# Linear attention, routed experts and a gated layer in one kernel: compact attention state, keys transposed after scaling, fewer spare zones zeroed, w_out's first words loaded into the slot's row tile

## The chip, the cores and the metric

The kernel runs on one core of a Trainium2 chip. The metric is device time of one execution in microseconds (us). TensorE is called PE, VectorE DVE, ScalarE ACT, GpSimd POOL, and SyncE SP; SP issues nearly all DMAs of this kernel, POOL the indirect ones.

## The reference

Three layers follow one another on 3072 tokens (4 batches of 768), with 384 features each:

```python
# 1: attention with a decaying state, 8 heads of 48
for t in range(S):
    cur = einsum('bhd,bhe->bhde', u * k[t], v[t])
    y[t] = einsum('bhd,bhde->bhe', r[t], state + cur)
    state = w[:, :, None] * state + einsum('bhd,bhe->bhde', k[t], v[t])
# 2: one of 8 experts for each token
e_idx = argmax(x @ w_gate + modality_bias[modality_id], axis=1)
out[mask] = gate_w[mask] * (relu(x[mask] @ w1[e]) @ w2[e])
# 3: gated layer with RMS norm
xn = x / sqrt(mean(x * x) + 1e-6) * rms_g
out = (silu(xn @ w_gate) * (xn @ w_val)) @ w_out
```

The weights of layer 3 are 64-bit floats; the kernel reads their two 32-bit words and makes a high and a low part of 32 bits from them.

## The kernel before

**Attention** works on 24 tiles of 128 tokens (i = 0 to 23; batch i % 4, chunk i // 4). The step loop at L833 is a software pipeline written out by hand: step s_ takes the state of tile s_-2 (`a_state`), transposes r and k of tile s_+1 (`a_T`, PE) and scales them with powers of w (`a_scale`, DVE), loads tile s_+4, multiplies keys with rows for tile s_ (`a_A`, PE), masks them (`a_mask`, DVE), forms y of tile s_-1 and the state's increment (`a_Y`, PE, copy on ACT), prepares the diagonal of tile s_+2 (`a_diag`, DVE, then eight ACT instructions), products with k for tile s_+3 (`a_rk`, `a_kp`, POOL), and turns y of tile s_-2 into token rows with gate logits (`a_X`). The order on PE, DVE, ACT, POOL and SP within the loop is that of the code. `soft()` puts the next small DVE instruction of routing behind an attention instruction; `hard()` drains what is left of it and issues the rank matmuls.

State `St[b]` is 128 partitions by 8 heads by 64, with each second head's half of the partitions zero, so that `pair(St[b], q)` is a full 128 by 128 matrix (L755). It is updated in two halves of 64 partitions: two DVE adds (L782) and two POOL products (L784). Keys are transposed unscaled from the padded load buffer (L718) and scaled by DVE out of PSUM (L726). `kpad` holds the keys times `Qt`, which POOL makes at L696 for the state's increment. Heads are padded from 48 to 64, and the pad columns are cleared by POOL.

**Hand-over to the experts.** `a_X` writes a token's row into one of six tiles `x` (L659). Routing finds, three tiles at a time, each token's place in the table `xs` in HBM, and POOL scatters one tile a step (`send_one`, L242). `xs` has for each expert 800 spare rows (`ZONE`) ahead of its tokens, which must read as zero when an expert's last slot reaches into them. SP writes zeros there during the step loop: the dummy zone in step 3, and one expert's zone in every second step from 5 to 19 (`zero_rows`, L257), 9 in all.

**Experts** work on slots of 792 tokens: two early slots, whose expert is known after 15 tiles, two more that are always computed, and a loop for any further ones. SP reads a slot's rows into `xslot` (L552), ACT scales them by the gate (L560), PE transposes them, and w1 and w2 come in chunks of 256 through three buffers each (L541, L543). A list of PE steps sets the order (one up and one down matmul group for a block of 128 hidden units and half a slot); from step 13 on pieces of layer 3's weights are decoded beside it (`decode`, L269). y goes to `ys` in HBM.

**Layer 3** (`glu`, L1095) takes blocks of 512 tokens: `gather` reads them from `ys` into `z`, `norm` scales them, `gv` makes the gated product for 128 hidden units, `o_mm` multiplies with w_out. In the first block, w_out's chunk f-1 is decoded in turn f; its words are loaded two turns ahead into a two-buffer staging tile, from the entry of `glu` on (L1148). z has one buffer; the next block's norm is spread over turns 1 to 10, its first ACT squares standing behind turn 1.

Of the kernel before, what the change touches and what calls it, by code (L numbers as in the profile page):

```python
# [24 lines left out]
E = 8  # L25
# [15 lines left out]
G = 3  # L41
EARLY_T = 15
# [14 lines left out]
def moe_chain_kernel(ctx: ExitStack, tc: tile.TileContext, r, k, v, w, u, mod, wgate, mbias,  # L57
# [34 lines left out]
    def pad_tile(nm, n, pool):  # L92
# [5 lines left out]
        P.memset(t[:, :, D:64], 0.0)  # L98
# [148 lines left out]
    def body(fast):  # L247
        with ExitStack() as st:
            moe = ExitStack()
            mp = moe.enter_context(tc.tile_pool(name="mp", bufs=2))  # L250
            zrow = {}

            def zero_rows(e):
                if not zrow:
                    zrow[0] = tabs[0:ZONE // 10, KD * HALF:KD * HALF + XW]
                    P.memset(zrow[0], 0.0)
                d = SP.dma_start(out=xs[e * STRIDE:e * STRIDE + ZONE, :].rearrange("(p t) d -> p t d", t=10),  # L257
                                 in_=zrow[0].rearrange("p (t d) -> p t d", t=1).to_broadcast([ZONE // 10, 10, XW]))
                if e < E:
                    tc.declare_no_dep(d.ins, group="xs", reason="rows that no token has")  # L260
                    tc.add_to_no_dep_group("xs", d.ins)
# [50 lines left out]
            def route(g, ls, xt):  # L312
# [40 lines left out]
                bk = bank(7, "rank")  # L353
                rk = bk[:, 0:G * E]
                T.matmul(rk, tri16, M.rearrange("p g e -> p (g e)"), start=True, stop=False)
                T.matmul(rk, ones16, C[:, 0:G, :].rearrange("p g e -> p (g e)"), start=False, stop=True)
                if (g + 1) * G in (EARLY_T, NT):
                    T.matmul(bk[0:1, 128:128 + E], ones16[:, 0:1], C[:, G, :], start=True, stop=True)
# [12 lines left out]
                if (g + 1) * G in (EARLY_T, NT):  # L371
                    cnt = p.tile([1, E], F32, name="cntf")
                    V.tensor_copy(cnt, bk[0:1, 128:128 + E])
# [133 lines left out]
            def slot_memory():  # L507
# [4 lines left out]
                return r1, r2, mp.tile([SUB, NSUB, XW], F32, name="xslot", bufs=1)  # L512

            raws1, raws2, xrows = slot_memory()
# [135 lines left out]

            def a_X(i):
# [6 lines left out]
                if fast:  # L658
                    x = xt[i] = ap.tile([128, XW], F32, name="x", bufs=6)  # L659
# [627 lines left out]
```

## Time and profile before

| what | us |
|---|---|
| median of 3 runs (lowest, highest) | 906.7 (905.68, 914.93) |
| the profiled execution | 903.63 |
| its span, first to last instruction | 901.8 |
| PE busy | 828.4 (92%) |
| DVE, ACT, POOL busy | 478.5, 332.8, 267.5 |
| mean granted PE clock | 0.968 |

The profile is of one execution. A line of the trace gives the start in us from the span's start, the duration, the engine, the line of the kernel, the operation and its output and inputs; in brackets stand the engine's idle time ahead of it and what ended it. PE's matmuls overlap, so the distance between starts says more than a duration. The granted clock is 1.00 at 2.4 GHz, and 0.50 at 1.2 GHz. The DMA share is the mean busy share of the 16 DMA engines.

### The profile page before, as it was taken

The numbers are of one execution on the slowest core, as the hardware profiler recorded it, in microseconds if no ns is written. First come the engines' busy times: TensorE is split into PE (matmuls) and PEld (weight loads), VectorE is DVE, ScalarE is ACT, GpSimd is POOL, SyncE is SP. The second block draws the span as 40 slices with busy tenths as digits, with TensorE's granted clock in tenths as the row PEclk, the third lists the DMA queues.
The fourth block names the chain that finished last, engine by engine and source line by source line (L and its number), as shares of the span: only waits on it lengthen the run. The fifth ranks groups of instructions, "written<-read, shape, count | busy, mean of one in ns | idle before, by whom it ended". The sixth has DMA issues, their size and how long they took to land.

```text
span 901.8 us, 13427 instructions
## 1 busy us (share of the span) xinstructions
PE 828.4 (92%) x5097; PEld 751.5 (83%) x5097; DVE 478.5 (53%) x969; ACT 332.8 (37%) x731; POOL 267.5 (30%) x314
## 2 busy tenths in 40 slices
PE   6996686988999999999699999999999999999995
PEld 5885576878989899999587888888888888888885
DVE  8985667848565787654178635324423423532121
ACT  3563244554655546543333331231222223122111
POOL 6453445634334234322154430120111013011001
PEclk9998798989999999999899999999999999999998
DMA  9999685275574364560711200110100010000001
GB/s 133 186 210 215 144 207 145 90 193 148 175 243 134 121 203 119 115 113 30 117 54 55 86 36 1 36 36 1 34 28 9 1 36 36 1 1 35 1 1 39
DMA packets 120831, 80.40 MB, mean 89 GB/s; under 512 B 85142, under 2 KB 111534, under 8 KB 120750
## 3 DMA queue, kind: packets, MB, share of 16 engines
q1 hardware_dynamic: 117470, 69.91, 32.6%
q0 software_dynamic: 3072, 9.46, 2.9%
q8 instruction: 43, 0.70, 0.4%
q14 instruction: 38, 0.31, 0.2%
q10 hardware_dynamic: 208, 0.00, 0.0%
HBM read 53.91 MB, written 25.46 MB: 88 GB/s over the span
## 4 chain that ended last, share of the span: by engine, by line
PE 53%; DMA 13%; issue 13%; DVE 10%; ACT 5%; POOL 4%; SPq 0%; POOLq 0%; ACTq 0%; DVEq 0%
PE vb L1116 11%; PE gb L1116 11%; PE hp L611 8%; DMA xs<-x,pos_all 7%; PE ob L1131 4%; PE ob L1132 4%; PE ob L1130 4%; PE y L630 2%; PE y L631 2%; PE y L629 2%; DMA kpad<-k 1%; DMA raw<-moe_w_gate 1%; DVE w1l L53 1%; DVE Am L743 1%; PE xb L656 1%
## 5 line engine op out<-in xcount | busy, mean ns | idle before, releaser
L1120 DVE TENSOR_TENSOR sg<-sg,vb 128x512 f32<-128x512 f32 x72 | 49.5, 687 | 216.8 <-PE vb L1116 211.7
L1130 PE MATMUL ob<-woh,acth 128*128 128x384 f32 x288 | 97.7, 339 | 6.5 <-ACT woh L285 6.5
L1131 PE MATMUL ob<-wol,acth 128*128 128x384 f32 x288 | 98.2, 341 | 2.6 <-POOL wol L53 2.5
L1122 ACT ACTIVATE acth<-sg 128x512 fp32r<-128x512 f32 x72 | 45.5, 632 | 148.6 <-DVE sg L1120 148.6
L1132 PE MATMUL ob<-woh,actl 128*128 128x384 f32 x288 | 97.7, 339 | 0.0
L1119 ACT ACTIVATE sg<-gb 128x512 f32<-128x512 f32 x72 | 42.8, 595 | 132.3 <-PE gb L1116 132.3
L711 ACT ACTIVATE Am<-ident,cd 128x128 f32<-128x128 f32 x184 | 56.4, 389 | 53.4 <-DVE cd L704 53.4
L611 PE MATMUL hp<-xh,w1h 128*128 128x396 f32 x192 | 68.5, 357 | 3.8 <-DVE hl L616 2.2
L242 POOL DMA_INDIRECT out<-room,toks x24 | 23.2, 966 | 155.1 <-ACT room L1141 84.3
L611 PE MATMUL hp<-xh,w1l 128*128 128x396 f32 x192 | 66.5, 346 | 2.4 <-DVE w1l L53 2.4
L611 PE MATMUL hp<-xl,w1h 128*128 128x396 f32 x192 | 66.2, 345 | 0.2 <-DVE xl L584 0.2
L630 PE MATMUL y<-hl,w2h 128*128 128x396 f32 x192 | 65.6, 342 | 0.8 <-DVE hl L616 0.8
L629 PE MATMUL y<-hh,w2h 128*128 128x396 f32 x192 | 65.6, 341 | 0.3 <-ACT hh L614 0.3
L631 PE MATMUL y<-hh,w2l 128*128 128x396 f32 x192 | 65.7, 342 | 0.0
L53 DVE TENSOR_TENSOR actl<-sg,acth 128x512 fp32r<-128x512 f32 x60 | 41.5, 692 | 41.9 <-ACT acth L1122 41.9
L1130 PEld LDWEIGHTS ob<-woh,acth 128*128 128x128 f32 x288 | 54.6, 190 | 10.0 <-ACT woh L285 7.1
L1131 PEld LDWEIGHTS ob<-wol,acth 128*128 128x128 f32 x288 | 54.4, 189 | 7.7 <-POOL wol L53 5.3
L616 DVE SCALAR_TENSOR_TENSOR hl<-hp,hh 128x396 fp32r<-128x396 f32 x64 | 36.2, 566 | 40.5 <-ACT hh L614 40.5
L1132 PEld LDWEIGHTS ob<-woh,actl 128*128 128x128 f32 x288 | 54.5, 189 | 0.1
L614 ACT ACTIVATE hh<-hp 128x396 fp32r<-128x396 f32 x64 | 32.0, 499 | 44.8 <-PE hp L611 44.5
L656 PEld LDWEIGHTS xb<-tabs,yT 128*128 128x128 f32 x192 | 27.2, 217 | 24.1 <-DVE ls L668 12.8
L1116 PE MATMUL gb<-xh,wgh 128*128 128x512 f32 x108 | 42.5, 394 | 1.9 <-issue 1.9
(258 smaller groups left out, 2114.7 us busy)
## 6 DMA issues: line engine op xcount, KB each, us to landing
xs<-tabs SPq DMA_DIRECT2D x9, 1206.2 KB
room<-moe_w SPq DMA_DIRECT2D x26, 384.0 KB
raw<-moe_w SPq DMA_DIRECT2D x14, 384.0 KB
xslot<-xs SPq DMA_DIRECT2D x8, 597.1 KB
raw<-moe_w_gate SPq DMA_DIRECT2D x12, 384.0 KB
raw<-moe_w_val SPq DMA_DIRECT2D x12, 384.0 KB
z<-ys SPq DMA_DIRECT2D x6, 768.0 KB
raw<-moe_w_out SPq DMA_DIRECT2D x12, 384.0 KB
```

What stands on the lines that cost most here:

```text
L53: eng.tensor_tensor(out, a, h.bitcast(F32), op=ALU.subtract)
L611: T.matmul(hp[:, 0:HALF], l[:, kk, :], m[:, kk], start=(n == 0), stop=(n == 8))
L629: T.matmul(y, bh[:, sl], hh, start=(f == 0), stop=False)
L630: T.matmul(y, bh[:, sl], hl, start=False, stop=False)
L631: T.matmul(y, bl[:, sl], hh, start=False, stop=(f == NFE - 1))
L711: A.activation(am[i][:, h % 2, h // 2, :], ident, AF.Copy, scale=c_[:, h:h + 1])
L1116: T.matmul(dst, l, m[:, kk], start=(n == 0), stop=(n == 8))
L1120: V.tensor_tensor(sg, sg, vb, op=ALU.mult)
L1122: A.activation(ah, sg, AF.Copy)
L1130: T.matmul(ob[o][:, 0:DM], ah[:, sl], wo_h[f], start=(f == 0), stop=False)
L1131: T.matmul(ob[o][:, 0:DM], ah[:, sl], wo_l[f], start=False, stop=False)
L1132: T.matmul(ob[o][:, 0:DM], al[:, sl], wo_h[f], start=False, stop=(f == NF2 - 1))
```

## The change

St becomes 128 partitions by 4 head pairs by 64; it is updated on all partitions by one DVE and one POOL instruction, and y takes from it two 64 by 64 products a pair in place of one of 128 by 128. From tile 2 on PE transposes `kpad` (keys already scaled), and ACT copies the result out of PSUM. Loaded keys then need no cleared pad beyond the first two buffers. y alternates between two PSUM banks; the increment s and the rank matmuls share bank 5. The ring of x rows has 10 tiles. Only the dummy zone is zeroed in the step loop; the zones of the two later slots' experts are zeroed when these slots are known. The words of w_out go into the memory of `xslot`, four chunks deep, and the first four are asked for during the last expert unit; the table for Silu is asked for at the entry of `glu`.

```diff
+XB = 10
...
-        P.memset(t[:, :, D:64], 0.0)
+        if nm != "k" or n < 2:
+            P.memset(t[:, :, D:64], 0.0)
...
+            xrow_t = xrp.tile([128, NSUB, XW], F32, name="xslot")
+            raw_o = xrow_t.rearrange("p t d -> p (t d)")[:, 0:8 * DM].bitcast(I32)
...
+            def zero_zone(sl):
+                SP.dma_start(out=xs[0:E * STRIDE, :].rearrange("(e n) d -> e n d", e=E)[bass.ds(sl.e, 1), 0:ZONE, :]
+                             .rearrange("o (p t) d -> p (o t) d", t=10), in_=zsrc)
...
+            def wo_load(f):
+                SP.dma_start(out=raw_o[:, f % 4], in_=o2w[f * 128:(f + 1) * 128, :].rearrange("p (n two) -> p n two", two=2))
...
-                bk = bank(7, "rank")
-                rk = bk[:, 0:G * E]
+                rk = aux[:, A_RK:A_RK + G * E]
...
-                    x = xt[i] = ap.tile([128, XW], F32, name="x", bufs=6)
+                    x = xt[i] = ap.tile([128, XW], F32, name="x", bufs=XB)
...
-                St = [ac.tile([128, H, 64], F32, name=f"St{b}") for b in range(B)]
+                St = [ac.tile([128, NP, 64], F32, name=f"St{b}") for b in range(B)]
...
+                        src = padded(nm, i) if nm == "r" or i < 2 else kpad[i % 5]
                         for q in range(NP):
-                            T.transpose(tb[:, q * 128:(q + 1) * 128], pair(padded(nm, i), q), ident)
+                            T.transpose(tb[:, q * 128:(q + 1) * 128], pair(src, q), ident)
...
-                        V.tensor_tensor(t, tb.rearrange("p (q n) -> p q n", q=NP), tab, op=ALU.mult)
                         tr[i].append(t)
-                        soft()
+                        if nm == "kT" and i >= 2:
+                            A.activation(t.rearrange("p q n -> p (q n)"), tb, AF.Copy)
+                        else:
+                            V.tensor_tensor(t, tb.rearrange("p (q n) -> p q n", q=NP), tab, op=ALU.mult)
+                            soft()
...
-                    y = bank(4, "y")
+                    y = bank(7 if i % 2 else 4, "y")
                     if c:
                         for q in range(NP):
-                            T.matmul(y[:, q * 128:(q + 1) * 128], pair(St[b], q), rT[:, q, :],
-                                     start=(q == 0), stop=False, skip_group_check=True)
+                            for hf in range(2):
+                                sl = slice(64 * hf, 64 * hf + 64)
+                                T.matmul(y[sl, q * 128:(q + 1) * 128], St[b][sl, q, :], rT[sl, q, :],
+                                         start=(q == 0), stop=False, skip_group_check=True)
...
-                        for n in range(2):
-                            rows = slice(64 * n, 64 * n + 64)
...
+                            tmp = ap.tile([128, NP, D], F32, name="stmp")
+                            V.tensor_tensor(tmp, sp, sf, op=ALU.add)
+                            soft()
+                            P.tensor_tensor(sf, tmp, decay, op=ALU.mult)
...
                     if s_ == 3:
-                        zero_rows(E)
-                    if 5 <= s_ < 5 + 2 * E and s_ % 2:
-                        zero_rows((s_ - 5) // 2)
+                        zero_row()
+                        zero_dummy()
...
                         slots.append(slot_new(rt["tabR"], j))
+                        zero_zone(slots[-1])
...
+                if n == len(units) - 1 and q == 6:
+                    for i in range(4):
+                        wo_load(i)
...
+                    A.activation(warm, ones[0:1, 0:1], AF.Silu)
...
-                    wo_load(0)
-                    wo_load(1)
                     gather(1)
...
-                        for _ in decode(raws.pop(f), wo_h[f], wo_l[f], DM):
+                        for _ in decode(raw_o[:, f % 4], wo_h[f], wo_l[f], DM):
                             pass
-                        if f + 2 < NF2:
-                            wo_load(f + 2)
+                        if f + 4 < NF2:
+                            wo_load(f + 4)
```

SP's queue in the step loop, around steps 3 to 5, before (L104 loads r, k and v of a tile, `room` and the names with `pad` are their buffers; L257 writes zeros to a zone of `xs`):

```order
L257 DMA xs<-tabs 800x1x386
L104 DMA rpad_203<-r 128x8x48
L104 DMA kpad_205<-k 128x8x48
L104 DMA room<-v 128x8x48
L104 DMA room<-r 128x8x48
L104 DMA room<-k 128x8x48
L104 DMA vpad_201<-v 128x8x48
L257 DMA xs<-tabs 800x1x386
L104 DMA room<-r 128x8x48
```

and with the change, the same place of SP's queue:

```order
L265 DMA xs<-tabs 800x1x386
L106 DMA rpad_206<-r 128x8x48
L106 DMA kpad_208<-k 128x8x48
L106 DMA room<-v 128x8x48
L106 DMA room<-r 128x8x48
L106 DMA room<-k 128x8x48
L106 DMA vpad_204<-v 128x8x48
L106 DMA room<-r 128x8x48
L106 DMA room<-k 128x8x48
```

The dummy zone stays, and the zone after six more loads is gone; so it is seven more times in the loop.

SP's queue in the second expert unit, before (`tabfb` is the table of the later slots, L541 and L543 load chunks of w1 and w2, L643 writes y of half a slot):

```order
L541 DMA raw_0_177<-moe_w 128x3x256
L543 ISA
L543 DMA raw_0_178<-moe_w 128x2x384
L526 TENSOR_LOAD tabfb
L526 ISA x2
L526 TENSOR_LOAD tabfb
L526 ISA x2
L541 ISA
L541 DMA room<-moe_w 128x3x256
L643 DMA ys<-tabs 128x3x396
L543 ISA
L543 DMA room<-moe_w 128x2x384
```

and with the change, the same place:

```order
L557 DMA raw_0_182<-moe_w 128x2x384
L540 TENSOR_LOAD tabfb
L540 ISA x2
L269 ISA
L269 DMA xs<-tabs 800x1x386
L657 DMA ys<-tabs 128x3x396
L540 TENSOR_LOAD tabfb
L540 ISA x2
L269 ISA
L269 DMA xs<-tabs 800x1x386
L555 ISA
L555 DMA room<-moe_w 128x3x256
```

Two zones of zeros now stand ahead of the next chunk of w1 (`room`), and so does the write of `ys`, which followed that chunk before.

ACT at the end of the step loop, before (`Am` is the diagonal, x a row tile, yT the copy of y, and the `xslot` rows scale the first slot's rows by the gate):

```order
L711 ACTIVATE Am<-ident,cd 128x128 x8
L660 ACTIVATE x<-xb 128x384
L591 ACTIVATE w1h<-raw_0_177 128x384
L762 ACTIVATE yT<-y 128x512
L600 ACTIVATE w2h<-raw_0_178 128x384
L660 ACTIVATE x<-xb 128x384
L591 ACTIVATE w1h<-raw_0_177 128x384
L762 ACTIVATE yT<-y 128x512
L560 ACTIVATE xslot<-xslot 99x384 x4
L660 ACTIVATE x<-xb 128x384
```

and with the change:

```order
L748 ACTIVATE kT<-kTp 128x512
L605 ACTIVATE w1h<-raw_0_181 128x384
L614 ACTIVATE w2h<-raw_0_182 128x384
L605 ACTIVATE w1h<-raw_0_181 128x384
L787 ACTIVATE yT<-y 128x512
L729 ACTIVATE Am<-ident,cd 128x128 x8
L678 ACTIVATE x<-xb 128x384
L748 ACTIVATE kT<-kTp 128x512
L574 ACTIVATE xslot<-xslot 99x384 x4
L787 ACTIVATE yT<-y 128x512
L678 ACTIVATE x<-xb 128x384
L787 ACTIVATE yT<-y 128x512
```

kT stands ahead of each yT. Four of the slot's eight scalings, which stood behind the last yT before, have moved up ahead of the yT of tile 21.

## Rows read from the trace of the kernel before

**Rows 1.** Busy time by window: engines, granted clock, DMA share and GB/s
```profile
core 0: us, PE busy (x) PEld busy (x) DVE busy (x) ACT busy (x) POOL busy (x), PEclk, DMA share, GB/s
0.00:24.40 24.40, 16.17 (x138) 13.69 (x138) 21.47 (x51) 8.66 (x25) 13.78 (x40) 0.94 0.95 135
24.40:60.00 35.60, 33.03 (x436) 30.13 (x437) 32.51 (x88) 21.71 (x66) 18.83 (x28) 1.00 1.03 199
60.00:101.50 41.50, 27.10 (x312) 24.67 (x309) 21.44 (x58) 13.58 (x41) 13.42 (x20) 0.86 0.98 208
...
161.00:174.00 13.00, 13.00 (x166) 11.78 (x164) 12.33 (x38) 6.81 (x21) 9.18 (x13) 0.99 0.41 136
...
220.00:236.00 16.00, 14.86 (x82) 14.86 (x83) 11.50 (x30) 8.74 (x19) 4.57 (x5) 1.00 0.92 275
```

**Rows 2.** DMA issues by line: engine, operation, count, size of one
```profile
xs<-tabs SPq DMA_DIRECT2D x9, 1206.2 KB
```

**Rows 3.** Who waited for whom, 24 to 188 us: total, times, longest
```profile
POOL St L784 <- DMA xs<-x,pos_all: 42.8, 9, 9.1
...
ACT x L660 <- DMA xs<-x,pos_all: 28.6, 8, 7.5
...
PE xb L656 <- DVE ls L668: 12.0, 6, 5.9
PE rank L356 <- DVE C L342: 11.3, 6, 2.3
```

**Rows 4.** The tile x, 24 to 188 us: its scatters from issue to landing
```profile
DMA to landing us min/median/max: 2.7/5.9/10.8
```

**Rows 5.** Timeline of PE, one step of attention without waits
```profile
163.76 1.14 PE L656 MATMUL xb<-tabs,yT 128*128 128x104 f32 x8
...
165.71 0.37 PE L736 MATMUL Aa<-rT,kT 64*128 64x128 f32 x1
...
166.59 0.27 PE L736 MATMUL Ab<-rT,kT 64*128 64x128 f32 x1
166.80 1.16 PE L755 MATMUL y<-rT,St 128*128 128x128 f32 x8
167.88 1.09 PE L759 MATMUL y<-Am,room 128*64 128x128 f32 x16
...
169.36 0.36 PE L656 MATMUL xb<-tabs,yT 128*128 128x104 f32 x1
```

**Rows 6.** The chain that ended last, one round through DVE and ACT
```profile
41.87 0.60 DVE kT L726
...
42.56 1.26 DVE Am L743 x2
...
44.88 2.45 ACT Am L711 x8
47.32 0.39 ACT x L660
...
47.73 0.19 DVE ls L668
```

**Rows 7.** Timeline of PE: y of tiles 1 and 23, rank, first expert matmul
```profile
24.41 1.23 PE L759 MATMUL y<-Am,room 128*64 128x128 f32 x16
...
187.26 1.09 PE L759 MATMUL y<-Am,vpad 128*64 128x128 f32 x16
190.72 0.17 PE L355 MATMUL rank<-M,tri 128*128 128x24 bf16 x1 [2.37 <-DVE M L333]
...
195.07 0.70 PE L611 MATMUL hp<-xh,w1h 128*128 128x396 f32 x1 [0.54 <-DVE xl L584]
```

**Rows 8.** Timeline of PE and ACT at the start of layer 3
```profile
447.70 0.69 PE L1130 MATMUL ob<-woh,acth 128*128 128x384 f32 x1 [6.52 <-ACT woh L285]
448.75 0.63 ACT L908 ACTIVATE n<-z 128x512 f32<-128x512 f32 x1 [1.10 <-DMA z<-ys]
...
450.33 0.57 ACT L1119 ACTIVATE sg<-gb 128x512 f32<-128x512 f32 x1
```

More of the change, by code (lines that the diff above doesn't have):

```diff
@@ L249, in body, with zero_row, zero_dummy @@
             moe = ExitStack()
+            xrp = st.enter_context(tc.tile_pool(name="xrp", bufs=1))
+            xrow_t = xrp.tile([128, NSUB, XW], F32, name="xslot")
+            raw_o = xrow_t.rearrange("p t d -> p (t d)")[:, 0:8 * DM].bitcast(I32)
+            raw_o = raw_o.rearrange("p (f n two) -> p f n two", n=DM, two=2)
             mp = moe.enter_context(tc.tile_pool(name="mp", bufs=2))
[L251 to L261, printed above, removed]
+            zrow = tabs[0:ZONE // 10, KD * HALF:KD * HALF + XW]
+            zsrc = zrow.rearrange("p (t d) -> p t d", t=1).to_broadcast([ZONE // 10, 10, XW])
+            def zero_row():
+                P.memset(zrow, 0.0)
+            def zero_dummy():
+                SP.dma_start(out=xs[DUMMY:DUMMY + ZONE, :].rearrange("(p t) d -> p t d", t=10), in_=zsrc)
+            def zero_zone(sl):
+                SP.dma_start(out=xs[0:E * STRIDE, :].rearrange("(e n) d -> e n d", e=E)[bass.ds(sl.e, 1), 0:ZONE, :]
+                             .rearrange("o (p t) d -> p (o t) d", t=10), in_=zsrc)
             def dec_load(src, n):
@@ L511, in slot_memory @@
                 r2 += [roomf[:, 768 * n:768 * n + 768].rearrange("p (o d) -> p o d", o=2) for n in (2, 3)]
-                return r1, r2, mp.tile([SUB, NSUB, XW], F32, name="xslot", bufs=1)
-            raws1, raws2, xrows = slot_memory()
+                return r1, r2
+            raws1, raws2 = slot_memory()
+            xrows = xrow_t[0:SUB]
             ysbs = [t[:, 0:KD * HALF].rearrange("p (k n) -> p k n", k=KD) for t in (tabs, power)]
@@ L649, in body @@
             yt, xt, ls = {}, {}, {}
+            aux = bank(5, "aux")
+            A_RK, A_CNT = 2 * NP * D, 2 * NP * D + G * E
             def a_X(i):
@@ L697, in a_kp @@
                     if i < B:
[L698 removed]
+                        P.memset(St[i][:, :, D:64], 0.0)
                 def a_diag(i, dg):
@@ L763, in a_Y @@
                     if c < NC - 1:
-                        sb[i] = bank(5, "s")
+                        sb[i] = aux[:, i % 2 * NP * D:(i % 2 + 1) * NP * D]
                         for q in range(NP):
@@ L772, in a_state @@
                         b = i % B
-                        sp = sb.pop(i)[:, 0:NP * D].rearrange("p (q d) -> p q d", q=NP)
+                        sp = sb.pop(i).rearrange("p (q d) -> p q d", q=NP)
                         decay = PT[:, :, 128:129].to_broadcast([128, NP, D])
-                        for n in range(2):
-                            rows = slice(64 * n, 64 * n + 64)
-                            sf = St[b].rearrange("p (q two) d -> p two q d", two=2)[rows, n, :, 0:D]
-                            if i < B:
-                                V.tensor_tensor(sf, sp[rows], decay[rows], op=ALU.mult)
-                            else:
-                                tmp = ap.tile([128, NP, D], F32, name=f"stmp{n}")[rows]
-                                V.tensor_tensor(tmp, sp[rows], sf, op=ALU.add)
-                                soft()
-                                P.tensor_tensor(sf, tmp, decay[rows], op=ALU.mult)
+                        sf = St[b][:, :, 0:D]
+                        if i < B:
+                            V.tensor_tensor(sf, sp, decay, op=ALU.mult)
+                        else:
+                            tmp = ap.tile([128, NP, D], F32, name="stmp")
+                            V.tensor_tensor(tmp, sp, sf, op=ALU.add)
+                            soft()
+                            P.tensor_tensor(sf, tmp, decay, op=ALU.mult)
             else:
                 def a_row(i):
-                    t = xt[i] = ap.tile([128, XW], F32, name="x", bufs=6)
+                    t = xt[i] = ap.tile([128, XW], F32, name="x", bufs=XB)
                     P.tensor_copy(t[:, DM + 1:XW], tokid[:, i:i + 1])
@@ L882, in body @@
                         for kk in range(KD):
-                            slot_x(slots[0], 0, kk, bank((0, 1, 5)[kk], "xtp"))
+                            slot_x(slots[0], 0, kk, bank((0, 1, 2)[kk], "xtp"))
                     if s_ == 1:
@@ L1089, in overflow @@
                                 unit_down(un, f, h)
+                    for i in range(4):
+                        wo_load(i)
                     gather(0)
```

20 lines of the change are left out of this document (10 added, 10 removed).

## The prediction

> **What bounds the kernel now.** I read the windows first, since the page's 92% for PE is an average. In attention PE is not full: from 24 to 60 us it is busy 33.0 of 35.6 us, from 60 to 101.5 only 27.1 of 41.5, with a granted clock of 0.86 (so partly at the lower of its two levels) and a DMA share of 0.98 [rows 1]. In a stretch without large transfers, from 161 to 174, it is full at clock 0.99 and the DMA share is 0.41 [rows 1]. Of the 73 us of the span in which PE is idle, 25 lie in the first three of these windows; after attention PE sets the time with few gaps.
>
> Next I read who waited for whom. ACT stood 28.6 us in 8 waits ahead of its copy into a row tile x until a scatter out of x had landed, and POOL's second half of the state 42.8 us [rows 3]. The scatters take 2.7 us at best, 5.9 in the median and 10.8 at worst to land [rows 4]. By the code x has six tiles, and tile i - 6 is scattered only one step before x of tile i is written: of each landing, all beyond one step is seen. ACT stops, and DVE's reduction ls behind it, and PE's next xb (12.0 us) [rows 3]. POOL's 42.8 is put down to the DMA, but what it needs is DVE's sum, which stands in the same queue: it is the same wait seen twice and not added.
>
> A step without waits takes 169.36 - 163.76 = 5.60 us on PE: xb with the transposes 1.95, key products 1.09, state product 1.08, masked product with the increment 1.48 [rows 5]. A second round is nearly as long: masks at 42.56, eight diagonals on ACT, the copy into x, the reduction at 47.73 [rows 6]: 5.2 us from masks to reduction and some 0.1 more to the next masks.
>
> **The change, part by part.** My zero is the profiled execution: 903.6 us, span 901.8. The median is 906.7, 3.1 above it.
>
> *Ring of ten.* The copy into tile i now waits for the scatter of i-10, sent five steps or about 28 us before; the slowest landing was 10.8 [rows 4]. The 28.6 us go. What is late next is the step itself, by PE or the round of rows 6.
>
> *Zones.* Eight of nine zone writes of 1206 KB [rows 2] leave the loop. Their price: to 24.4 us only loads ran, 0.95 × 24.4 = 23.2 us of share for 135 GB/s × 24.4 = 3.3 MB, or 16.8 loads of 197 KB (128 × 8 × 48 floats), 1.38 us a load. From 24.4 to 60 us three zones were issued; 1.03 × 35.6 = 36.7 us of share carried 7.1 MB, of which 3.7 are zones and 3.4, or 17 loads, cost 23.8; that leaves 4.3 us a zone. The same sum from 60 to 101.5 us, where three scatters ran too, gives 3.4 [rows 1]. So about 31 us of transfers leave. A step's three loads need 4.1 us, with a scatter between 4.5 and 5: below 5.6, so the engines should no longer hold the step.
>
> *State and keys.* DVE loses the key scaling (0.6 us [rows 6]) and one of two sums; POOL one of two products; ACT gains one 128x512 copy, 0.6 us by an ACT row of that size [rows 8]. On ACT it stands between the copy into x and the diagonals, where ACT waits for DVE's masks and sums; their 44.88 - 42.56 = 2.3 us [rows 6] cover it, and yT. If PE's transposes came late, up to 0.6 a step would show. Moving keys behind POOL's product adds a wait for PE, with POOL's load, product and scatter queue ahead of it; by the code kpad of tile i is made in step i-3 and transposed in i-1, two steps or 11 us of cover. The state product becomes 8 half products in place of 4 full ones, 16 PE passes for 8. No row shows 64 by 64 ones. The key products have 64 rows each, and 16 passes take 1.09 us because pairs start together; the masked products, halves by columns, take 0.93 [rows 5]. If pairs run together the new ones take 0.9 to 1.1 us against 1.08; one after the other, at 0.135 a pass, 2.16. I take no change, nearest to the key products; the bounds are -0.2 and +1.1 on 20 tiles, -4 and +22 us.
>
> The row that comes nearest has its two row halves in two banks, Aa and Ab [rows 5]; here both halves of y go to one bank. The Trainium skill, TensorEngine Tiling (Array Packing), Gotcha 1: PSUM Pressure, says: "Different row tiles cannot access same PSUM bank simultaneously". No run here shows a pair of row halves in one bank. By that rule the halves follow one another and the step takes 6.7 us; this is rival B.
>
> *Sum for attention.* The first 24.4 us stay: loads and DVE fill them (21.5 of 24.4) [rows 1]. From y of tile 1 to tile 20 there are 19 steps of 5.6, 106.4 us. The last three need no loads ahead and lose transposes, products and increments one by one; put together from the pieces of rows 5 they take 5.05, 4.1 and 3.0, together 12.1. The six rank groups cost 11.3 us of waits for DVE's counts [rows 3]; DVE is less full, but with fewer soft places more of routing is drained ahead of the rank matmul, so I keep 0.5 each, 3 us. y of tile 23 comes at 24.4 + 106.4 + 12.1 + 3.0 = 145.9, against 187.3 [rows 7]: -41.4. From there to the first expert matmul it is 7.8 us now, 2.4 of them a wait for a route that was late for the same scatter [rows 7]: -2.4. Against that, four slot scalings now stand on ACT ahead of a yT one step after the slot's rows are asked for. They need tile 14's scatter (2.7 or more [rows 4]) and 1.2 MB of rows (as a zone, 3.4 to 4.3), 7 us against a step and a half, 8: 0 to 4 us, I take 2. Attention: -41.8.
>
> *Zones in the expert stage.* Two zone writes come in the second unit, ahead of a w1 chunk on SP, where the DMA share is already 0.92 [rows 1]. Between 0, if three chunk buffers cover them, and 2 × 4.3 = 8.6. The next chunk is wanted about 10 us after it is asked for now, and comes 4 us later from SP and behind 7 to 9 us of zeros; I take +3.5. Later slots read those zones some eight PE steps on.
>
> *w_out.* PE's first output matmul stood 6.5 us for ACT's woh [rows 8], which waited for the words. With the words there at once, the next late thing is z: ACT's squares of the norm wait until 448.75, and Silu of turn 2 stands behind them, at 450.33 [rows 8]; without it PE can't reuse the gate bank. PE does its output matmuls early and stops there. What is left is that z shares the engines with less. I take -1.5, within 0 and -6.5. The early Silu table lies beside PE's first matmuls: 0. The four loads, 1.6 MB, cost about as much share as a zone and a third, in the last expert unit, where PE is busy: 0, at worst +2.
>
> Sum: 903.6 - 41.8 + 3.5 - 1.5 = 863.8; with the median's 3.1, **867 us**.
>
> **Rivals.**
> A, the forecast: 867, own range 857 to 878.
> B, halves in turn: +1.08 us on each of 20 tiles on PE, which is the longer round then: 867 + 21 = 888. For it: no row pairs them in one bank. Against: column halves share a bank and pair.
> C, loads still hold the step: share falls to 4.6 of 5.6 us, but loads are asked for only one to two steps ahead. At 6.2 us a step, 22 × 0.6 = 13: 880. For it: DMA was full for 100 us. Against: even with zones, PE kept 33.0 of 35.6 us busy from 24 to 60.
> D, w_out's wait goes whole: 867 - 5 = 862. Against it speaks the Silu at 450.33.
> E, slower than before: keys wait for POOL. Each product stands behind its load, and PE's transposes behind it. It decides from the point where a step takes 5.6 + 39.8 / 22 = 7.4 us: if loads land 7 us later than asked in each step, more than the two steps of cover, with POOL's queue stopping scatters and state too. Then about 910. Against it: with zones gone, loads get quicker.
>
> **How the numbers follow.** A 0.62, B 0.17, C 0.13, D 0.05, E 0.03. The number is A's. From 855 (A's low end with a better state product) to 886 lie most of A, C and D and about half of B: 8 in 10. This kernel's runs can tell about 1% from no change, 9 us. All but E lie beyond that; I leave a little for mixtures: faster 0.95, same 0.02, slower 0.03.
>
> **What would show it.** ACT's copy into x no longer waits for scatters; PE's steps are 5.5 to 5.8 us from xb to xb, at clock 1.00; the first expert matmul starts near 153 us; the 16 passes of the state product span about 1.0 us. PE waits once for w1 in the second unit for some 3 us. In layer 3, PE waits ahead of turn 3's gate matmul, with z as the cause. State products of 2 us show B; POOL's product waiting for a load in most steps shows C or E; a first expert matmul after 165 us would make the forecast wrong.

## The result, and the profile after

The changed kernel takes 878.61 us in the median of four runs (875.93 to 884.64), the kernel before 910.21 us in the runs beside them: a ratio of 0.967, 95% interval [0.962, 0.973]. The forecast was 867 us with a range of 855 to 886. Faster was right, the range holds the time, and a fifth of the gain expected is missing: some 32 us less in the medians, where 40 were forecast.

The profiled execution of after has a span of 882.7 us (before: 901.8). It is the longest of its four runs, and the profiled execution of before (903.63) is shorter than any of the four beside it; so the two show only 19 us of the gain. By stage, from the starts of PE's first instructions of each (an expert matmul is here one of a group that makes `hp`, the hidden units):

| stretch | before | after | difference | forecast |
|---|---|---|---|---|
| start to first expert matmul | 195.1 | 162.3 | -32.8 | -41.8 |
| first expert matmul to the start of the last such group | 226.3 | 237.9 | +11.6 | +3.5 |
| from there to layer 3's first gate matmul | 6.9 | 7.1 | +0.2 | 0 |
| layer 3, first block | 83.3 | 83.6 | +0.3 | -1.5 |
| the rest | 390.2 | 391.8 | +1.6 | 0 |

Attention in windows, after (columns as in [rows 1]):

```profile
24.40:36.00 11.60, 9.66 (x135) 8.58 (x131) 9.59 (x21) 7.91 (x25) 5.13 (x8) 1.00 0.88 199
36.00:48.00 12.00, 7.73 (x84) 7.18 (x86) 6.61 (x15) 5.23 (x15) 4.72 (x6) 0.72 0.89 154
48.00:60.00 12.00, 11.79 (x176) 10.68 (x176) 9.96 (x35) 7.89 (x23) 5.02 (x7) 1.00 0.51 100
60.00:101.50 41.50, 40.90 (x597) 37.09 (x594) 30.98 (x92) 28.44 (x83) 27.79 (x38) 1.00 0.74 161
```

From 60 to 101.5 us PE is full at clock 1.00 where it was busy 27.1 us at 0.86 [rows 1]. One stretch went wrong: from 36 to 48 us PE is busy 7.73 of 12, and the mean granted clock is 0.72.

Who waited, after, 24 to 165 us (compare [rows 3]: no line names a scatter any more):

```profile
POOL St L807 <- DVE pf L374: 14.8, 5, 3.9
...
POOL dg L708 <- DMA kpad<-k: 7.6, 1, 7.6
...
PE y L784 <- DVE mT L228: 5.1, 1, 5.1
```

PE's timeline of that stretch, then of the loop's end (compare [rows 5, 7]):

```profile
40.27 1.97 PE L784 MATMUL y<-Am,vpad 128*64 128x128 f32 x16 [5.06 <-DVE mT L228]
...
43.00 1.89 PE L674 MATMUL xb<-tabs,yT 128*128 128x104 f32 x8
...
46.79 1.09 PE L780 MATMUL y<-rT,St 64*64 64x128 f32 x16
47.81 1.09 PE L784 MATMUL y<-Am,vpad 128*64 128x128 f32 x16
...
138.94 1.09 PE L784 MATMUL y<-Am,vpad 128*64 128x128 f32 x16
141.11 0.17 PE L366 MATMUL aux<-M,tri 128*128 128x24 bf16 x1 [1.07 <-DVE M L345]
142.72 0.17 PE L367 MATMUL aux<-C,ones 128*128 128x24 bf16 x1 [1.44 <-DVE C L354]
142.75 1.24 PE L674 MATMUL xb<-tabs,yT 128*128 128x104 f32 x8
143.78 1.06 PE L737 MATMUL rTp<-ident,rpad 128*128 128x128 f32 x4
...
162.30 0.70 PE L625 MATMUL hp<-xh,w1h 128*128 128x396 f32 x1 [0.68 <-DVE xl L598]
```

The masked product y of tile 3 (L784) waits 5.06 us for DVE's mT, which nothing in the forecast names. What stood ahead of mT in DVE's queue:

```profile
36.89 0.19 DVE L686 TENSOR_REDUCE ls<-xb 128x8 f32<-128x32 f32 x1 [1.66 <-ACT x L678]
...
38.21 1.33 DVE L719 TENSOR_TENSOR dg<-dg,tabs 128x384 f32<-128x384 f32 x1
39.58 0.55 DVE L722 TENSOR_REDUCE cd<-dg 128x8 f32<-128x384 f32 x1
40.05 0.17 DVE L228 COPY mT<-mps 128x24 f32<-128x24 f32 x1
```

mT is DVE's copy of the transposed modality ids `mps` out of PSUM bank 7, and y of odd tiles now has bank 7 too (`y = bank(7 if i % 2 else 4, "y")` in the diff). In DVE's order mT stands at the end of that step, behind the reduction `ls`, which waits for ACT's copy into x, behind the masks (at the cut) and behind the next diagonal; PE's y of tile 3 stands in the same step and needs the bank before.

POOL's product of that step is late as well:

```profile
38.13 0.99 POOL L708 TENSOR_TENSOR dg<-rpad,kpad 128x384 f32<-128x384 f32 x1 [7.56 <-DMA kpad<-k]
```

SP asked for its k tile at 29.90 us, right behind the dummy zone's zeros at 28.44. But it does not hold mT: DVE's `dg` starts at 38.21, while this product still runs, so it works on the one that POOL made a step earlier.

In the expert stage, the chain of waits that ended last, after (start, us, what):

```profile
196.38 9.09 DMA xs<-tabs
206.33 8.99 DMA room<-moe_w
230.67 13.51 DMA raw<-moe_w_val
344.53 10.16 DMA ys<-tabs
357.08 12.98 DMA raw<-moe_w_gate
```

The first line is a zone of zeros, the second the w1 chunk behind the other zone. The last two, a write of ys and a gate chunk, stand in SP's queue behind the early words of w_out: SP issues these at 327.7 to 341.4 us, one unit earlier than the code suggests. The code's order binds PE, DVE, ACT and POOL in the expert stage, not SP.

At the start of layer 3, after, PE waits for w_out's low part and then for the gate bank, which ACT frees only behind its squares of z (compare [rows 8]):

```profile
424.18 0.69 PE L1162 MATMUL ob<-wol,acth 128*128 128x384 f32 x1 [3.05 <-POOL wol L54]
430.35 0.79 PE L1147 MATMUL gb<-xh,wgh 128*128 128x512 f32 x1 [2.28 <-ACT sg L1150]
```

```profile
428.15 0.63 ACT L930 ACTIVATE n<-z 128x512 f32<-128x512 f32 x1 [7.52 <-DMA z<-ys]
```

### The profile page after: what moved, and what is told of

Read it like the earlier page. It is cut to its first block, busy times and chain, and to the rows that moved or that the text cites. A ratio compares the mean times of both kernels' runs of the same rounds, so it can differ in the third digit from the quotient of the medians.

```text
span 882.7 us, 13678 instructions
## 1 busy us (share of the span) xinstructions
PE 827.4 (94%) x5257; PEld 746.9 (85%) x5257; DVE 456.2 (52%) x927; ACT 341.9 (39%) x754; POOL 257.0 (29%) x296
## 4 chain that ended last, share of the span: by engine, by line
PE 57%; issue 12%; DVE 11%; DMA 10%; ACT 6%; POOL 2%; SPq 0%; ACTq 0%; DVEq 0%; POOLq 0%
PE gb L1147 12%; PE vb L1147 12%; PE hp L625 6%; PE ob L1162 4%; PE ob L1163 4%; PE ob L1161 4%; PE xb L674 3%; DMA ys<-tabs 2%; PE y L784 2%; PE Aa L759 2%; PE y L644 2%; PE y L645 2%; PE y L643 2%; DMA raw<-moe_w_val 2%; PE y L780 2%
## 5 line engine op out<-in xcount | busy, mean ns | idle before, releaser
L643 PE MATMUL y<-hh,w2h 128*128 128x396 f32 x192 | 66.1, 344 | 5.1 <-ACT hh L628 5.1
L244 POOL DMA_INDIRECT out<-room,toks x24 | 23.2, 966 | 156.2 <-ACT room L1172 84.8
L54 DVE TENSOR_TENSOR actl<-sg,acth 128x512 fp32r<-128x512 f32 x60 | 41.5, 692 | 42.0 <-ACT acth L1153 42.0
L625 PEld LDWEIGHTS hp<-xh,w1h 128*128 128x128 f32 x192 | 37.2, 194 | 7.2 <-DVE hl L630 4.9
```

Of the source, the lines that this page charges most:

```text
L625: T.matmul(hp[:, 0:HALF], l[:, kk, :], m[:, kk], start=(n == 0), stop=(n == 8))
L643: T.matmul(y, bh[:, sl], hh, start=(f == 0), stop=False)
```

## The experiments

Medians are in us; a ratio is to the kernel before on the same chip, with its 95% interval. "Hp" is the start of the first expert matmul in the profiled execution, "stage" the expert stage of the table above. Both are of one execution each: wout_late and wout_undone, which leave attention as in the changed kernel, have Hp at 161.1 and 159.9, against its 162.3. So a difference of some 2 us in Hp says little.

### What freed attention: ring, state or zones?

**ring_only**, the kernel before with `bufs=6` of `x` made `bufs=10`.

> The kernel before with ten row tiles in place of six; nothing else differs. Theory ring: ACT's 28.6 us of waits for scatters go, the loads still share the DMA engines with the zones; 20 to 28 us less than before, 880 to 888. Rival loads: with the zones in the loop the loads of r, k and v are late as well, and take over as soon as ACT no longer waits: 5 to 15 us less, 893 to 903, with PE or POOL waiting for loads between 60 and 101 us.

Measured: 904.74, ratio 0.9985 [0.9944, 1.0026]; Hp 191.9 (before: 195.1). Both theories fall. ACT's waits for scatters are gone, and almost nothing is gained. POOL's, which the forecast had put down as the same wait seen twice, are still there; 24 to 170 us:

```profile
POOL St L784 <- DMA xs<-x,pos_all: 25.4, 6, 7.4
```

One of them on POOL's timeline, and the same stretch in the chain of waits:

```profile
101.80 1.16 POOL L242 DMA_INDIRECT xs<-x,pos_all  x1 [0.15 <-issue]
...
103.11 0.52 POOL L784 TENSOR_TENSOR St<-stmp,power 64x192 f32<-64x192 f32 x1
111.03 0.51 POOL L784 TENSOR_TENSOR St<-stmp,power 64x192 f32<-64x192 f32 x1 [7.41 <-DMA xs<-x,pos_all]
111.62 1.00 POOL L690 TENSOR_TENSOR dg<-room 128x384 f32<-128x384 f32 x1
```

```profile
101.80 9.07 DMA xs<-x,pos_all
...
111.06 0.48 POOL St L784
...
111.62 1.01 POOL dg L690
...
112.66 1.34 DVE dg L701
```

DVE had made the sum for that product by 103.3 us. POOL stood for the scatter it had itself sent in that step, and `dg`, with DVE, ACT and PE behind it, waited too. The order of POOL's instructions with the semaphores that each waits for, in the kernel before, says the same of every step from the first scatter on:

```
71 L242 DMA xs<-x,pos_all 31776x386 [waits Activation_49]
72 L661 COPY x<-tokid 128x1
73 L784 TENSOR_TENSOR St_194<-stmp_1009,power 64x4x48 [waits DVE_49]
74 L784 TENSOR_TENSOR St_194<-stmp_1014,power 64x4x48 [waits DMASW1_49,DVE_49,Pool_49]
```

The product for the second half of the state (partitions 64 to 127) waits for a scatter's semaphore (`DMASW`). In the changed kernel the one product on all partitions waits for `DVE_49` and `Pool_49` alone. Why the half product got that wait no run shows.

**ring_back**, the changed kernel with `XB = 10` made `XB = 6`.

> The changed kernel with the ring of row tiles at six again, as before; nothing else differs. Theory ring (as the prediction has it): a scatter that lands later than one step after it is sent stops ACT, 28.6 us of such waits before the change; most comes back, 15 to 28 us, total 893 to 906. Rival zones: the scatters landed late only because the zones of zeros stood ahead of them on the DMA engines; with the zones gone from the loop they land in about 3 us, within the step, and six tiles do: 0 to 5 us, total 878 to 884.

Measured: 878.83, ratio 0.9695 [0.9635, 0.9753]; Hp 158.4. The rival's numbers come out: the ring is worth nothing in the changed kernel either (POOL does wait 8.0 us for scatters there, in 4 waits ahead of x, and nothing shows of it). Its reason is half of the matter, as the next four runs show.

**state_only**, the kernel before with the compact state alone:

```diff
-St = [ac.tile([128, H, 64], F32, name=f"St{b}") for b in range(B)]
+St = [ac.tile([128, NP, 64], F32, name=f"St{b}") for b in range(B)]
...
-for n in range(2):
-    rows = slice(64 * n, 64 * n + 64)
...
+sf = St[b][:, :, 0:D]
...
+P.tensor_tensor(sf, tmp, decay, op=ALU.mult)
```

> The kernel before with the compact state alone (one sum on DVE, one product on POOL, 16 half products on PE, no wait of the state product for a scatter); keys, ring of six, nine zones in the loop and w_out as before. Theory state: POOL's 42.8 us of waits ahead of the state product go, though ACT's and POOL's waits for the ring of six can take part of them back: 15 to 30 us less than before, 878 to 893. Theory zones: the loads and scatters stay late, 0 to 10 us less, 898 to 908.

Measured: 881.45, ratio 0.9710 [0.9656, 0.9765]; Hp 169.0. Theory state's numbers: with nine zones in the loop and six row tiles, this part alone brings nearly the whole gain. It does not end every wait for a scatter. POOL's copy of a token id into x, which needs the tile that an older scatter reads, now waits (24 to 170 us):

```profile
POOL x L661 <- DMA xs<-x,pos_all: 20.7, 6, 4.9
```

zones_back below, with ten row tiles, has no such wait. A ring of ten with only the compact state beside it was not tried, nor the full state without the semaphore; the compact state also saves a sum on DVE and a product on POOL in each step.

**zones_out**, the kernel before without the eight zone writes:

```diff
-if 5 <= s_ < 5 + 2 * E and s_ % 2:
-    zero_rows((s_ - 5) // 2)
```

> The kernel before without the eight zone writes (it leaves the spare zones unwritten; the ninth, of rows for no slot, stays); state, keys, ring and w_out as before. Theory zones: scatters land in about 3 us, POOL's and ACT's waits for them shrink to a few us, attention loses 20 to 35 us: 873 to 888. Theory state: POOL still waits in every step for the scatter just sent, 2 to 4 us a step, and a step takes 6.5 to 8 us: 5 to 12 us less than before, 896 to 903.

Measured: 883.47, ratio 0.9732 [0.9678, 0.9787]; Hp 169.6. POOL's waits are still there, ten of them, but short:

```profile
POOL St L784 <- DMA xs<-x,pos_all: 18.2, 10, 3.0
```

Theory zones' numbers, and so this part alone brings nearly the same as the other. The two do not add: they are two cures of one wait. Either POOL no longer waits for the scatter that it has just sent, or that scatter lands early enough (3.5 us in the median here, 5.9 before).

**state_full**, the changed kernel with the full state (state_only's diff the other way round).

> The changed kernel with the full state array again (128x8x64, zeros beside each head, 8 full state products, two sums on DVE and two products on POOL a step); keys, ring, zones and w_out as changed. By the order of instructions POOL's product for the second half of the state then waits for the scatter that POOL sent just before it, as in the kernel before, and in the changed kernel no state product waits for a scatter. Theory state (POOL's queue stands behind each scatter's landing): POOL's waits ahead of the state product come back at 2 to 4 us a step even without zones, POOL's round of scatter, landing, state product, two products and the next scatter takes 6.5 to 8 us, and attention grows by 15 to 30 us: 892 to 908. Theory zones (scatters land late only because of the zones): without them a scatter lands in about 3 us, POOL's round stays at or under 6 us, and 0 to 6 us come back: 878 to 885.

Measured: 888.83, ratio 0.9783 [0.9730, 0.9836]; Hp 173.3, 11 us later than in the changed kernel. POOL's waits are back:

```profile
POOL St L807 <- DMA xs<-x,pos_all: 16.1, 7, 4.0
```

The total lies between the two theories' numbers. The mechanism is the state's; its size without zones is some 10 us in the medians. Not all of it is POOL's wait as such: of the 11 us in the trace 7 lie between y of tiles 22 and 23, where PE stands 5.3 us for a token row whose copy follows, on ACT, the scaling of the first slot's rows, and ACT waits 7.8 us for these.

**zones_back**, the changed kernel with the eight zone writes in the loop again:

```diff
+if 5 <= s_ < 5 + 2 * E and s_ % 2:
+    e_ = (s_ - 5) // 2
+    d = SP.dma_start(out=xs[e_ * STRIDE:e_ * STRIDE + ZONE, :].rearrange("(p t) d -> p t d", t=10), in_=zsrc)
...
-        zero_zone(slots[-1])
```

> The changed kernel with the eight zone writes in the step loop again and none in the expert stage; state, keys, ring and w_out as changed. Theory state: no engine waits for a scatter's landing any more, so the zones cost only what late loads of r, k and v cost: 0 to 10 us in attention, less 2 to 4 us won back in the second and third expert unit: 876 to 886. Theory zones: the DMA engines are full again from 24 to 101 us and loads and scatters come late; 15 to 28 us come back, 893 to 906.

Measured: 876.40, ratio 0.9665 [0.9607, 0.9723]; Hp 164.8, stage 228.4 (changed kernel: 162.3 and 237.9). Theory state holds. The window that was the forecast's witness against the zones:

```profile
60.00:101.50 41.50, 39.81 (x585) 36.00 (x581) 31.21 (x87) 27.65 (x80) 26.77 (x36) 1.00 1.00 225
```

The DMA engines are at 1.00 of their time for 41.5 us, and PE is busy 39.81 of them. In this kernel the zones in the loop cost the total nothing that can be seen; Hp is 2.5 us later. In the expert stage the two waits in the second and third unit, 3.8 us together in the changed kernel, are gone. The stage is 9.5 shorter in all: 2.4 more are won in its first 27 us, where the granted clock was 1.00 over the first 10 us and 0.74 in the changed kernel's profile, and 3.0 in the last unit, which comes up again under w_out.

### What held attention back

**bias_bank**, the changed kernel with one line changed:

```diff
-y = bank(7 if i % 2 else 4, "y")
+y = bank(7 if i % 2 and i != 3 else 4, "y")
```

> The changed kernel with the product y of tile 3 put in the PSUM bank of the even tiles; nothing else differs. In the changed kernel y of tile 3 stands 5.1 us (35.2 to 40.3 us) ahead of PE, and the next passes run at the lower clock. Theory bank: the second bank of y is also the one in which the transposed modality ids lie until DVE has copied them, and DVE does that only behind a product that waits for a late load of k; without the shared bank y of tile 3 starts before 37 us, the half-clock passes at 40 to 45 us go, and the first expert matmul comes 3 to 6 us earlier (156 to 159 instead of 162.3): about 873 to 876 us. Rival load: the late k, behind the zeros of the spare zone on the DMA engines, holds DVE and POOL anyhow; y of tile 3 starts early, but y of tile 4 still comes at 46 to 48 us, and the first expert matmul stays within 1.5 us of 162.3: about 878.

Measured: 877.98, ratio 0.9694 [0.9635, 0.9753]; Hp 156.5 instead of 162.3. The same product, with no wait and at full clock:

```profile
32.97 1.09 PE L784 MATMUL y<-Am,vpad 128*64 128x128 f32 x16
...
35.07 1.14 PE L674 MATMUL xb<-tabs,yT 128*128 128x104 f32 x8 [0.56 <-DVE ls L686]
```

Theory bank holds for the shared bank and for its 5.8 us in the trace (3.4 to 4.6 against the two other profiles with the changed kernel's attention). Its total, 873 to 876, was not reached: the median is 0.6 below the changed kernel's, well inside the interval. Its account of why mT is late, a late load of k, falls. Here POOL's product of that step comes later still, and DVE has copied mT before it starts:

```profile
37.20 0.17 DVE L228 COPY mT<-mps 128x24 f32<-128x24 f32 x1
```

```profile
38.56 1.01 POOL L708 TENSOR_TENSOR dg<-rpad,kpad 128x384 f32<-128x384 f32 x1 [7.16 <-DVE biasT L236]
```

**keys_plain**, the changed kernel with the keys as before:

```diff
-src = padded(nm, i) if nm == "r" or i < 2 else kpad[i % 5]
+src = padded(nm, i)
...
-if nm == "kT" and i >= 2:
-    A.activation(t.rearrange("p q n -> p (q n)"), tb, AF.Copy)
...
+V.tensor_tensor(t, tb.rearrange("p (q n) -> p q n", q=NP), tab, op=ALU.mult)
+soft()
```

> The changed kernel with the keys transposed unscaled and scaled by DVE on the way out of PSUM, as before; compact state, ring, zones and w_out as changed. Theory keys-idle (DVE has room: 31.0 of 41.5 us busy from 60 to 101 us): DVE's extra 0.68 us a step lies beside PE's work, the step stays at 5.5 to 5.6 us, the total within 3 us of the changed kernel: 875 to 882. Rival keys-DVE (the round through DVE's masks, ACT's diagonals and DVE's reduction is as long as PE's step, and 0.68 more on DVE is seen): a step of 6.0 to 6.3 us between 60 and 139 us, 7 to 10 us more: 885 to 889.

Measured: 874.31, ratio 0.9619 [0.9576, 0.9661]; Hp 156.6. The rival falls; the step stays at 5.5 us, and undoing this part is if anything a gain (the interval overlaps the changed kernel's). Behind y of tile 20, where the changed kernel waits 1.07 and 1.44 us for routing:

```profile
135.46 1.09 PE L780 MATMUL y<-Am,vpad 128*64 128x128 f32 x16
136.49 0.19 PE L365 MATMUL aux<-M,tri 128*128 128x24 bf16 x1
137.58 0.17 PE L366 MATMUL aux<-C,ones 128*128 128x24 bf16 x1 [0.91 <-DVE C L353]
137.61 1.12 PE L673 MATMUL xb<-tabs,yT 128*128 128x104 f32 x8
138.56 0.60 PE L736 MATMUL rTp<-ident,rpad 128*128 128x128 f32 x4
```

The DVE scaling carries a `soft()`, behind which one more piece of routing goes out in each step. Without it routing's M comes later, PE waits, and its transposes then run at the lower clock, 1.06 us (143.78 above) in place of 0.60. That the lost soft place alone does this was not tried by itself. It is also not the whole of the 5.7 us: 3.1 are there by y of tile 4 (44.7, and 47.8 in the changed kernel), since y of tile 3 waits 3.06 for mT in place of 5.06; 3.2 are won between tiles 20 and 21, and 2.3 of them lost again between 22 and 23, where ACT's scaling of the slot's rows waits 4.12 us for them.

**best2**, keys_plain and bias_bank together.

> Two edits together on the changed kernel: keys transposed unscaled and scaled by DVE, and y of tile 3 in the bank of the even tiles; state, ring, zones and w_out as changed. Theory of parts: each took 5.7 us of the first expert matmul's start by itself (162.3 to 156.6 and to 156.5 us); if they are different waits both go, the first expert matmul starts at 150 to 154 us and the total is 866 to 871. Rival same wait: both act on the same stall between y of tiles 2 and 3 (11.2 us in the changed kernel, 8.0 and 4.9 with either edit), and the second adds nothing: first expert matmul at 155 to 157 us, 872 to 876.

Measured: 872.75 (868.72 to 875.01), ratio 0.9628 [0.9588, 0.9667]; Hp 152.9. In the trace both gains are there, as theory of parts says; the total lies just inside the rival's range. This is the lowest median of all kernels here, but its interval overlaps the changed kernel's: better than before is shown, better than the change is not.

### The expert stage and w_out

**wout_late**, the changed kernel with the four early loads of w_out at the start of layer 3:

```diff
-if n == len(units) - 1 and q == 6:
-    for i in range(4):
-        wo_load(i)
...
+for i in range(4):
+    wo_load(i)
 gather(1)
```

> The changed kernel with the first four w_out loads asked for at the start of layer 3, into the same tile, in place of the last expert unit; nothing else differs. In the changed kernel SP issues them at 327.7 to 341.4 us, the write of ys issued at 344.5 lands only at 354.9, and SP's next write waits for that, with chunks of w2 and of the gate weights behind it. Theory queue: that wait is the 10.0 us gap between two expert matmuls at 366.3 to 376.3 us and the 4.5 us one behind it; without the loads the gaps are 4.8 and 3.3 as before the change, and the expert stage (first expert matmul to last) takes 231 to 232.5 us instead of 237.9. Theory queue with layer 3 unharmed: total 872 to 874. Rival back: the expert stage shrinks by 6, but PE's wait for woh in layer 3 (6.5 us before the change) comes back, and the total stays at 877 to 880. Rival chunk: the gate chunk took 12 to 13 us to land before the change too, so the gap stays at 9 to 10 us and the stage at 237 to 238.

Measured: 880.30, ratio 0.9738 [0.9673, 0.9804]; stage 231.7, layer 3's first block 86.7. The stage shrinks by 6.2, as theory queue says, but only 3.3 of it are in the last unit's first gap (5.2 us above the kernel before, now 1.9); 2.4 are won in the first 27 us, at a granted clock of 1.00 in place of 0.74 over the first 10, long before these loads. The first block grows by 3.1, and the total doesn't fall: rival back.

**wout_undone**, the changed kernel with the whole w_out part undone:

```diff
+wo_load(0)
+wo_load(1)
 gather(1)
...
-for _ in decode(raw_o[:, f % 4], wo_h[f], wo_l[f], DM):
+for _ in decode(raws.pop(f), wo_h[f], wo_l[f], DM):
...
-if f + 4 < NF2:
-    wo_load(f + 4)
+if f + 2 < NF2:
+    wo_load(f + 2)
```

> The changed kernel with the w_out part undone: two raw tiles of their own, loaded from the start of layer 3, no early Silu table, the slot's row tile back in the expert pool; attention, zones and ring as changed. Theory z (the norm of z sets the start of layer 3, and the early loads only disturb the last expert unit): layer 3's first block (first gate matmul to the second block's) stays at 83 to 84 us, the gap between expert matmuls that was 10.0 us becomes 4.8 to 7, and the total is 1 to 5 us lower than the changed kernel's: 873 to 877. Rival words (the early words are worth something in layer 3): the first block grows to 85 to 90 us as PE waits for woh again, and the total is the same or up to 4 us higher: 878 to 882.

Measured: 876.96, ratio 0.9638 [0.9598, 0.9679]; stage 235.5, first block 84.8, rest 390.0 (changed kernel 237.9, 83.6, 391.8). The total is theory z's, the pieces are mixed: 1.3 lost in the first block, 1.8 won behind it, and the gap in the last unit is still 3.9 us above the kernel before. So the early loads are not that gap's only cause.

What the gap waits for is a gate chunk, and two times make it: until SP comes to that chunk, behind the first write of ys, and from there to its use. The first is 12.2 to 13.6 us in the seven profiles with the early loads, and 9.8 to 11.5 in the seven without them (9.9 in the kernel before, 12.6 in the changed kernel, 10.7 in wout_late, 11.5 here). So the early loads do cost there, some 2 us. The second is 10.9 to 13.1 us and follows neither edit. The gap itself, above the kernel before, is 2.2 in zones_back, which keeps the early loads, and 1.7 and 2.1 in state_only and zones_out, which never had them: the 3.3 of wout_late is little more than this spread, and the zones in the expert stage have a part in it too. How they reach a gap some 160 us later stays open.

In layer 3 the profiles agree better. The first block takes 83.3 to 86.0 us (mean 84.8) in the six with w_out as before, and 82.0 to 84.5 (83.3) in the seven with the words early. All that follows takes 389.5 to 390.3 in these six, and 391.3 to 391.8 in these seven and in wout_late. So the words win some 1.5 us and the w_out part loses as much behind the first block; why it does, no run shows.

**best1**, zones_back, bias_bank and wout_undone together.

> Three edits together on the changed kernel: the eight zone writes in the step loop again, y of tile 3 in the bank of the even tiles, the w_out part undone; compact state, keys and ring stay. Theory of parts: from 876.4 with the zones back alone, 3 to 5 us go with the wait of y of tile 3 and 0 to 3 with w_out: 868 to 873, with y of tile 3 before 37 us, the first expert matmul at 158 to 162 us and an expert stage of 226 to 228 us. Rival late loads: with the zones in the loop loads hold the first steps anyway, the first expert matmul stays at 163 to 165 us: 874 to 877.

Measured: 876.97, ratio 0.9632 [0.9584, 0.9680]; Hp 167.2, stage 227.1, y of tile 3 at 33.8. The expert stage is nearly as good as before the change, but Hp is 2.4 us later than in zones_back and 10.7 later than in bias_bank, whose loop has no zones. The total is the rival's, and so is its reason, though not for the first steps alone. POOL waits for loads of k (24 to 170 us), and PE, in the window of zones_back above, is less full:

```profile
POOL dg L700 <- DMA kpad<-k: 13.7, 4, 4.4
...
POOL dg L700 <- DMA room<-k: 11.4, 3, 5.0
```

```profile
60.00:101.50 41.50, 37.34 (x501) 33.81 (x500) 30.54 (x83) 23.91 (x69) 23.66 (x31) 0.92 0.99 220
```

Once y of tile 3 doesn't stand, the zones do cost attention something: the loads hold some of its steps.

## Why the prediction was right, and where it was wrong

**Ring of ten: wrong.** The step that failed is in the reading of the waits: "what it needs is DVE's sum, which stands in the same queue: it is the same wait seen twice and not added" of POOL's 42.8 us [rows 3]. The sum was done, and the profile had named the cause rightly. The 28.6 us that the forecast gave to the ring are worth 3.8 in the medians of ring_only, with no change inside its interval, and nothing in the changed kernel (ring_back). The gain is the compact state's or the zones', either one: 0.971 and 0.973 alone, 0.967 with both. That the number came out is in part luck: the forecast took the compact state for no change, and this edit ends, by itself, the wait of POOL that the ring leaves.

**Zones in the loop: the transfers right, the consequence half right.** They made the scatters late, and with that POOL; without POOL's wait a DMA share of 1.00 left PE nearly full (zones_back). Rival C, loads that hold the step, falls for the changed kernel: 0.74 and PE at 40.90 of 41.5. With the zones in the loop it has a point (best1).

**The step and the state product: right.** From y of tile 4 at 47.8 to tile 20 at 138.9 there are 16 steps in 91.1 us, 5.7 each with the rank waits; the forecast had 5.60 and 0.5 a rank group. The 16 half products take 47.81 - 46.79 = 1.02 us, against 1.08 expected. Rival B falls: two row halves that write one bank, in different partitions, ran as pairs here, their starts 0.007 us apart. The Trainium skill, TensorEngine Tiling (Array Packing), Gotcha 1: PSUM Pressure, says that different row tiles cannot use one bank at the same time. The trace does not agree, and the measurement decides.

**The sum for attention: right in sign, 9 us too good.** y of tile 23 came at 155.7, not 145.9. 6.6 us were lost by tile 4 (47.8 against 24.4 + 3 × 5.6 = 41.2): the second bank of y, an edit of the diff that the forecast didn't price, and the half-clock passes behind its wait; in bias_bank y of tile 4 comes at 39.1. 4.5 were lost between tiles 20 and 21 (9.5 against 5.05). The forecast had named the cause, "with fewer soft places more of routing is drained ahead of the rank matmul", and priced it at 0.5 a group: the steps with the five groups before took 0.4 to 0.8 more than the others, but the last group was mis-sized. The tail from there to the first expert matmul, 6.6 us, was forecast as 7.4: the 2 us put there for the slot scalings do not show in the changed kernel, where ACT waits 1.79 for the rows and PE does not; in keys_plain and state_full they do.

**Keys: cover right, price too low.** The copy on ACT is covered, and the step stayed; the lost soft place, priced at 0.5 a group, shows at the last one, as far as keys_plain can tell.

**Zones in the expert stage: right in size, partly by other waits.** +3.5 was forecast, and 3.8 stand in two waits that zones_back doesn't have. The first is 1.2 us at the second unit's w1, where the forecast had its 3; the other, 2.6, is a w_val chunk 13.51 us under way, which it hadn't named. The second wait stands in all eight profiles with the zones there and in none of the six others. The stage as a whole grew by 11.6, and most of the rest is the last unit's gap, 5.2.

**w_out: right on z, wrong on the loads.** -1.5 was forecast for the first block of layer 3, with z as the next late thing. Z is: the gate matmul at 430.35 waits for Silu behind the squares of z. The pair of profiles shows no gain (83.3 and 83.6), all profiles together some 1.5; but PE's 3.05 for POOL's low part of w_out was not named, and the 1.7 lost behind the first block neither. The four loads in the last unit were to cost "0, at worst +2". The step that failed is their place: SP issues them a unit earlier, ahead of a write of ys for whose landing SP then waits, with two chunks behind it. That costs SP some 2 us; how much of the last unit's gap is theirs stays open, up to 3.3 by wout_late.

The range held because these errors, nearly all of one sign, stayed small. The mechanism that the forecast put first was not the one.

## What to carry to other kernels

When two engines wait for the same DMA, ask the program's own waits before calling one of them the other's shadow: freeing one is worth nothing while the second, in its own queue, still stands. Read every edit of a diff for the resource that it newly shares (here a PSUM bank with an early transposition), and look up where a DMA is issued, not where the code has it. Before a wait is put down to a late load, compare the start of the instruction that is said to need it with the end of the one that makes its data. Two parts that each remove the same wait must not be added, and the second may then only bring its own costs.

## What the runs showed of the hardware that was not expected

- A DMA share of 1.00 at 225 GB/s for 41.5 us left PE busy for 39.81 of them (zones_back). A share of 0.99 went with 37.34 where POOL waited for loads (best1), and one of 0.98 with 27.1 where it waited for scatters [rows 1].
- A wait of 5.06 us on PE cost more than its length: the passes behind it ran at the lower of the two clock levels (0.50 granted from 40.2 to 42.0 us), y in 1.97 us against 1.09 and xb in 1.89 against 1.14, 1.6 us more.
- Sixteen 64 by 64 products, pairs of row halves in one PSUM bank, took 1.02 us.
- A 384 KB chunk that SP issues behind a write of ys and a chunk of w2 took 11 to 13 us from its issue to its use, in all fourteen profiles.
